# Gated attention and its feed-forward layer on one core: outputs split into a part by state and a part by scores, with the instruction order rebuilt

## The chip, the core and the metric

The kernel runs on one core of a Trainium2 chip. The core's engines are TensorE (PE in the profile; its weight loads are PEld), VectorE (DVE), ScalarE (ACT), GpSimd (POOL) and SyncE (SP), which issues all DMAs here. The metric is the device time of one execution in microseconds (us). Matmuls write to PSUM, which has eight banks; a bank is 512 fp32 wide on each of 128 partitions.

## What is computed

A gated linear attention over 4 batches, 8 heads, 768 steps and head size 48, then a feed-forward layer on the 3072 x 384 result:

```
for t in range(S):
    state = alpha[:, :, t, :, None] * state + np.einsum('bhd,bhe->bhde', k[:, :, t], v[:, :, t])
    y[:, :, t] = np.einsum('bhd,bhde->bhe', q[:, :, t], state)
...
h = x @ w_in                       # 3072 x 384 by 384 x 2048
g = np.where(pos, h, np.where(neg, 0.0, (h + beta) ** 2 / (4.0 * beta)))
return (g @ w_out).astype(np.float32)   # 3072 x 2048 by 2048 x 384
```

The two weight matrices come as 64-bit floats, the rest as fp32.

## The kernel before

**Chunks.** The steps are cut into 24 chunks of 128 (`NCH`; j counts them, six to a batch). A chunk is cut again into two halves u of 64 steps, and the 8 heads into 4 pairs g of two heads r. Head r of a pair lies on partitions 64r to 64r+47 (`low[r]`).

**Preparing a chunk** (`prepare`). SP loads alpha, k, q (L508 whole for the first `EARLY` chunks, L526 in four pieces for the later ones) and v (L577). The first `EARLY` chunks are transposed by the PE (L542, into PSUM), the later ones by DVE (L555). Two scans on DVE (L632, L658) make the decays, and products with them make Q (L678) and K (`inv`, L672).

**Attention of a chunk** (`begin_chunk`, `attend`). The PE transposes K (L699), and ACT copies the result to `ks` (L702). Three kinds of small fp32 matmuls follow, each on a part of the 128 x 128 array:

- `update` (L727): k^T v of a half u; rows of half u of the array, columns of head r, so the four quarter tiles of 64 x 64 take one each. A chunk that ends a batch has u = 0 alone.
- `scores` (L714): K with Q; rows of head r, columns of half u, again four quarter tiles.
- `outputs` (L854): the stationary operand is 128 rows of `both`, in which the state of a head (48 rows) and v (64 rows) lie above each other; the moving operand is Q for r = 0 and `other` for r = 1, each holding q on the rows of the state and masked scores on the rows of v. So each uses half of the array (all rows, 64 columns), and one matmul sums both parts.

Between them DVE multiplies the scores with the causal mask into the free rows of Q and `other` (L800, four of 64 partitions a chunk; for the first `HELP` chunks two of them go over ACT L772 and POOL L782), ACT copies Q's half into `other` (L764), DVE adds the update to `state` (L756), POOL decays it (L831), and ACT or POOL copies it into `both` (L746, L749), twice for each half. The output is then split into an fp32r high and low part in `ring` (L878 on ACT, L883 on DVE). From j = 7 (`MERGE`) the PE does update(j), scores(j) and outputs(j-1) as one burst; before that they are separate.

**Feed-forward** (`hidden`, `second`). Chunks go in groups of three (`GROUP`). A row f of a group is 128 of the 2048 hidden units: 9 matmuls of 128 x 384 (L950), the activation on ACT, DVE and POOL (L979, L994, L1005, L1009, L1010), and 9 matmuls (L1028). There are 8 groups of 16 rows f, so 128 rows L950 and 128 rows L1028, each counted here as one row of work. The first two groups take the first half of f before the second half. Weights come in eight pairs (SP L460, L470, L480) and are decoded to fp32r parts by ACT, DVE and POOL (L372 to L427). L994 is left out, and three ACT operations stand in its place, where a row's key is under `CLIPS`.

**What sets the order.** `Plan` records every operation with a duration, a key (its due time) and its operands, then places them engine by engine with its own costs of matmul modes, DMAs and waits, and emits the program in that order. Where it expects the PE to idle early on, it puts dummy matmuls in (L1099, `fill`). The constants at the top of the file steer it. Each engine works through its own row in that order.

## Time and profile before

| | |
|---|---|
| median of 3 runs | 530.55 us (530.52 to 531.27) |
| the profiled execution | 533.23 us, of which the profile's span is 531.5 us |
| PE busy by line, us (instructions, each of L714, L727 and L854 shown twice) | L1028 226.2 (x1152), L950 226.3 (x1188), L854 27.0 and 26.9 (x372 each) and 2.6 and 2.6 (x36 each), L714 16.6 (x768), L727 16.5 (x704), L1099 16.3 (x109), L699 14.7 (x96), L542 6.2, 6.1 and 5.9 (x36 each) |
| POOL, longest line | L1010 137.9 (x129) |
| DMA | 53.88 MB, 112241 packets, 77392 of them under 512 B |

The page of the profile gives busy time and share of the span for each engine, then the span in 40 slices (13.3 us each), the chain of work that ended last, and the groups of instructions by line with their mean duration. Matmuls overlap in the pipeline, so a row's duration is longer than the time from one matmul's start to the next.

### The profile page before, as it was taken

The numbers are of one execution on the slowest core, as the hardware profiler recorded it, in microseconds if no ns is written. First come the engines' busy times: TensorE is split into PE (matmuls) and PEld (weight loads), VectorE is DVE, ScalarE is ACT, GpSimd is POOL, SyncE is SP. The second block draws the span as 40 slices with busy tenths as digits, with TensorE's granted clock in tenths as the row PEclk, the third lists the DMA queues.
The fourth block names the chain that finished last, engine by engine and source line by source line (L and its number), as shares of the span: only waits on it lengthen the run. The fifth ranks groups of instructions, "written<-read, shape, count | busy, mean of one in ns | idle before, by whom it ended". The sixth has DMA issues, their size and how long they took to land.

```text
span 531.5 us, 12796 instructions
## 1 busy us (share of the span) xinstructions
PE 509.8 (96%) x4943; PEld 488.6 (92%) x4943; DVE 387.5 (73%) x709; ACT 281.0 (53%) x548; POOL 270.7 (51%) x327
## 2 busy tenths in 40 slices
PE   8888899999999999999999999999999999999995
PEld 6777789889989999999999999999999999999995
DVE  6799988778989896778686896688696884333331
ACT  3777898999845443434444543444444534334332
POOL 4656789879954443443543552543453552333330
PEclk9999999999999999999999999999999999999999
DMA  9999847892535733345324433345334210101001
GB/s 154 203 213 206 175 102 150 186 206 73 152 87 130 201 79 92 91 83 130 96 60 96 124 98 82 90 84 134 90 68 97 74 26 2 23 1 44 1 2 49
DMA packets 112241, 53.88 MB, mean 101 GB/s; under 512 B 77392, under 2 KB 107056, under 8 KB 112176
## 3 DMA queue, kind: packets, MB, share of 16 engines
q1 hardware_dynamic: 112176, 53.01, 44.9%
q8 instruction: 41, 0.67, 0.6%
q14 instruction: 24, 0.20, 0.1%
HBM read 45.02 MB, written 5.90 MB: 96 GB/s over the span
## 4 chain that ended last, share of the span: by engine, by line
PE 75%; DVE 7%; POOL 7%; ACT 3%; DMA 3%; issue 3%; SPq 1%; DVEq 0%; POOLq 0%
PE ps L1028 32%; PE ps L950 30%; PE ps L854 5%; PE ps L727 2%; PE ps L714 2%; POOL wt L427 2%; POOL gh L1010 2%; PE ps L699 2%; DMA sums<-ot 2%; PE ps L1099 1%; PE ps L542 1%; ACT gf L979 1%; DVE Q L632 1%; SPq L899 1%; POOL w L412 1%
## 5 line engine op out<-in xcount | busy, mean ns | idle before, releaser
L1028 PE MATMUL ps<-wt,gh 128*128 128x384 f32 x1152 | 226.2, 340 | 5.7 <-POOL gh L1010 3.4
L950 PE MATMUL ps<-ring,wt 128*128 128x384 f32 (+1 forms) x1188 | 226.3, 336 | 1.7 <-DMA ring<-ring 1.0
L1010 POOL TENSOR_TENSOR gh<-gf,gh 128x384 fp32r<-128x384 f32 (+1 forms) x129 | 137.9, 1070 | 158.1 <-ACT gh L1009 123.8
L950 PEld LDWEIGHTS ps<-ring,wt 128*128 128x128 f32 x1188 | 205.2, 188 | 4.0 <-issue 1.0
L1028 PEld LDWEIGHTS ps<-wt,gh 128*128 128x128 f32 x1152 | 200.2, 188 | 8.8 <-POOL gh L1010 5.3
L979 ACT ACTIVATE gf<-gf,half_b 128x384 f32<-128x384 f32 x104 | 63.8, 617 | 108.2 <-DVE gf L994 106.8
L1009 ACT CAST gh<-gf 128x384 fp32r<-128x384 f32 (+1 forms) x132 | 66.3, 503 | 77.7 <-DVE gf L1005 68.5
L1005 DVE TENSOR_TENSOR gf<-gf,ps 128x384 f32<-128x384 f32 (+1 forms) x132 | 70.3, 535 | 43.1 <-ACT gf L979 41.3
L994 DVE TENSOR_SCALAR gf<-ps 128x384 f32<-128x384 f32 x104 | 57.1, 552 | 52.1 <-PE ps L950 49.6
L427 POOL TENSOR_TENSOR wt<-w,wt 128x384 fp32r<-128x384 f32 x31 | 34.4, 1124 | 2.2 <-ACT wt L425 1.7
L831 POOL TENSOR_TENSOR state<-state,last 128x192 f32<-128x192 f32 x20 | 12.7, 634 | 36.1 <-DVE state L756 35.9
L412 POOL TENSOR_TENSOR w<-w,wt 128x384 int32<-128x384 int32 x26 | 28.5, 1114 | 5.1 <-issue 3.0
L854 PE MATMUL ps<-other,both 128*64 128x64 f32 x372 | 27.0, 225 | 0.0
L854 PE MATMUL ps<-Q,both 128*64 128x64 f32 x372 | 26.9, 225 | 0.0
L800 DVE TENSOR_TENSOR Q<-ps,mask 64x256 f32<-64x256 f32 x48 | 20.3, 423 | 8.3 <-ACT other L764 6.0
L854 PEld LDWEIGHTS ps<-Q,both 128*64 128x64 f32 x372 | 23.5, 138 | 2.5 <-issue 1.1
L632 DVE TENSOR_TENSOR_SCAN Q<-turn,fwd 128x512 f32<-128x512 f32 x15 | 21.0, 1399 | 6.6 <-PE ps L854 6.5
L702 ACT COPY ks<-ps 128x512 f32<-128x512 f32 x24 | 14.0, 584 | 20.1 <-PE ps L699 20.1
L678 POOL TENSOR_TENSOR Q<-Q,turn 128x512 f32<-128x512 f32 x16 | 20.7, 1294 | 6.8 <-DVE turn L555 6.4
L854 PEld LDWEIGHTS ps<-other,both 128*64 128x64 f32 x372 | 23.5, 138 | 0.0
L641 POOL TENSOR_SCALAR last<-Q 128x4 f32<-128x4 f32 x24 | 6.6, 274 | 28.6 <-DVE Q L632 28.1
L746 ACT COPY both<-state 48x192 f32<-48x192 f32 x51 | 17.8, 349 | 5.4 <-POOL state L831 3.9
(93 smaller groups left out, 570.3 us busy)
## 6 DMA issues: line engine op xcount, KB each, us to landing
wt<-in_moe_w_out SPq DMA_DIRECT2D x8, 768.0 KB, 7.5
raw_a<-in_alpha SPq DMA_DIRECT2D x60, 96.0 KB, 2.3
raw_k<-in_k SPq DMA_DIRECT2D x60, 96.0 KB, 2.4
raw_q<-in_q SPq DMA_DIRECT2D x60, 96.0 KB, 2.2
vt<-in_v SPq DMA_DIRECT2D x24, 192.0 KB, 4.0
wt<-in_moe_w_in SPq DMA_DIRECT2D x16, 288.0 KB, 5.8
out<-ot SPq DMA_DIRECT2D x24, 192.0 KB, 2.4
both<-in_v SPq DMA_DIRECT2D x72, 48.0 KB, 2.5
```

What stands on the lines that cost most here:

```text
L412: add = lambda e, c=c: e.tensor_tensor(out=bits()[:, c], in0=bits()[:, c], in1=word(I32, 0)[:, c], op=ALU.add)
L427: sub = lambda e, c=c: e.tensor_tensor(out=part(1)[:, c], in0=data()[:, c], in1=part(0).bitcast(F32)[:, c], op=ALU.subtract)
L632: lambda: nc.vector.tensor_tensor_scan(flat(Q()), aT(), flat(fwd), 0.0, ALU.mult, ALU.max),
L678: mul = lambda e: e.tensor_tensor(out=flat(Q()), in0=flat(Q()), in1=qT(), op=ALU.mult)
L854: nc.tensor.matmul(out=ps()[halves[r], to, halves[u]], lhsT=lhsT[:, u, r], rhs=x()[:, g, halves[u]], start=m + u == 0, stop=True, skip_gro ...
L950: nc.tensor.matmul(out=h(), lhsT=win(f, w)[:, kt], rhs=ring[:, at, kt, a, :], start=(m == 0), stop=(m == 3 * KT - 1),)
L979: lambda: nc.scalar.activation(out=gf(), in_=in_(), func=func, scale=scale, bias=bias),
L994: lambda: nc.vector.tensor_scalar(out=gf(), in0=h(), scalar1=-1.0, scalar2=1.0, op0=ALU.max, op1=ALU.min),
L1005: lambda: nc.vector.tensor_tensor(out=gf(), in0=gf(), in1=h(), op=ALU.max),
L1009: plan.op("ACT", 0.08 + 0.41 * w, key + 0.4, lambda: nc.scalar.copy(out=gh()[:, 0], in_=gf()), [gf], [gh])
L1010: sub = lambda e: e.tensor_tensor(out=gh()[:, 1], in0=gf(), in1=gh()[:, 0].bitcast(F32), op=ALU.subtract)
L1028: nc.tensor.matmul(out=o_ps[seg][t](), lhsT=gh()[:, a, (t - c0) * CH : (t - c0 + 1) * CH], rhs=wout(f, w), start=(f == f0 and i == 0), sto ...
```

## The change

Outputs are made in two passes that add up in PSUM. By state: `st` (48 rows of head r) with Q as it lies, into the columns of the same head, so quarter tiles on the diagonal of the array. By scores: `vv` (v of a half, on the rows of the other head) with `T`, the masked scores, so quarter tiles off the diagonal. A drain of the PE stands between. `T` is written by one DVE instruction for all 128 partitions, the state is added straight into `st`, and the copies into `both` and `other` are gone. A burst now also exists inside the first two groups (`joined`). The constants of the planner are changed, and its row of every engine is made anew. In the diff a line of "..." marks what is left out.

```diff
-EARLY = 9
+EARLY = 7
 MORE = 2
-WARM = 10
+WARM = 15
...
-MARGIN1 = 6.0
+MARGIN1 = 3.0
...
-LATER = 4.0
+LATER = 1.0
...
-HELP = 4
 VHELP = 6
-SPLIT = 2
-CLIPS = 24.0
+SPLIT = 1
+CLIPS = 9.0
...
-    ISSUE, LAND, RATE = 0.42, 1.9, 190e3
+    ISSUE, LAND, RATE = 0.42, 1.4, 300e3
+    SMALL = 2.1
...
-            vec(0.1, lambda: nc.vector.tensor_copy(out=meet[:, j, 1], in_=inv()[:, :, 0]), [inv], [("meet", j, 1)], False)
+            vec(0.15, lambda: nc.vector.reciprocal(out=meet[:, j, 1], in_=inv()[:, :, 0]), [inv], [("meet", j, 1)], False)
...
+        def joined(j):
+
+            return j + 1 < NCH and (j >= MERGE or group_of[j] == group_of[j + 1])
...
         def scores(j):
             Q, K, _ = prepared[j]
...
+            return [
+                lambda g=g, r=r, u=u: nc.tensor.matmul(
+                    out=meets[j][0]().rearrange("p (g t) -> p g t", g=G)[halves[1 - r], g, halves[u]],
+                    lhsT=K()[low[r], g, halves[u]],
+                    rhs=Q()[low[r], g, halves[u]],
...
+        def update(j, u):
+
+            return [
+                lambda g=g, r=r: nc.tensor.matmul(
+                    out=up(j, u)[64 * r : 64 * r + 64, g],
+                    lhsT=turnt[j]()[halves[u], g, 64 * r : 64 * r + 64],
+                    rhs=V[j]()[halves[u], 2 * g + r],
...
+        def outputs(j, ps, x):
+
+            n, i = group_of[j], j % 2
+            moving = (prepared[j][0], others[j])[x]
+            parts = [((st, vv)[x][:, i, :, g], g, g) for g in range(KT if n == 0 else G)]
+
+            parts += [((rest_s, rest_v)[x][:, :, kt], KT, kt) for kt in range(KT) if n == 0]
+
+            def product(m, u, r):
+                lhsT, g, to = parts[m]
+                rows = halves[1 - r] if x else low[r]
+
+                return nc.tensor.matmul(
+                    out=ps()[halves[r], to, halves[u]],
+                    lhsT=lhsT[rows, u],
+                    rhs=moving()[rows, g, halves[u]],
+                    start=m + u + x == 0,
...
+            return [lambda m=m, u=u, r=r: product(m, u, r) for m in range(len(parts)) for u in range(2) for r in range(2)]
+
+        def both(a, b):
+
+            todo = []
+            for i in range(0, max(len(a), len(b)), 2):
+                todo += a[i : i + 2] + b[i : i + 2]
+            return todo
...
         def follow(j, key):
...
-            plan.op("ACT", 0.6, key - 0.1, lambda: nc.scalar.copy(out=other()[HC:], in_=Q()[HC:]), [Q], [other])
...
+            plan.op(
+                "DVE",
+                0.66,
+                key,
+                lambda: nc.vector.tensor_tensor(
+                    out=T().rearrange("p g (u t) -> p (g u) t", u=2),
+                    in0=meets[j][0]().rearrange("p (g t) -> p g t", t=HC),
+                    in1=mask2[:, None, :].broadcast_to([P, 2 * G, HC]),
+                    op=ALU.mult,
+                ),
...
-                def burst(ps=ps):
-                    update(j)
-                    scores(j)
-                    outputs(j - 1, ps)
...
+            def burst():
+                more = update(j, 1) if (j + 1) % PER else []
+                if not before:
+                    run(scores(j) + both(update(j, 0), more))
+                    return
+                run(both(outputs(j - 1, old, 0), scores(j)))
+                run(update(j, 0))
+                nc.tensor.drain()
+                run(both(outputs(j - 1, old, 1), more))
...
+                def by_state():
+                    run(outputs(j, ps, 0))
+
+                def by_scores():
+                    nc.tensor.drain()
+                    run(outputs(j, ps, 1))
...
+        nc.vector.reciprocal(out=meet[:, :, 1], in_=meet[:, :, 1])
```

On the PE, in the middle of the program: the burst of chunk 11 before, a chunk that ends a batch (vt with ks is `update`, Q with inv is `scores`, Q or other with both is `outputs`). These are the first rows of it, after a row of the feed-forward; the last two repeat to sixteen.

```order
L950 MATMUL ps<-ring,wt 128x384 x9
L727 MATMUL ps<-vt,ks 64x48 x8
L714 MATMUL ps<-Q,inv 64x64 x16
L854 MATMUL ps<-Q,both 64x64
L854 MATMUL ps<-other,both 64x64
```

On the PE of the changed kernel, the middle of a burst of a chunk that does not end a batch, up to the feed-forward after it (Q with st is the pass by state, T with vv the pass by scores; the drain, which the rows do not name, stands behind the eight updates):

```order
L770 MATMUL ps<-Q,st 64x64 x2
L732 MATMUL ps<-Q,inv 64x64 x2
L747 MATMUL ps<-vt,ks 64x48 x8
L770 MATMUL ps<-T,vv 64x64 x2
L747 MATMUL ps<-vt,ks 64x48 x2
L770 MATMUL ps<-T,vv 64x64 x2
L747 MATMUL ps<-vt,ks 64x48 x2
L770 MATMUL ps<-T,vv 64x64 x2
L747 MATMUL ps<-vt,ks 64x48 x2
L770 MATMUL ps<-T,vv 64x64 x2
L747 MATMUL ps<-vt,ks 64x48 x2
L770 MATMUL ps<-T,vv 64x64 x8
```

The first two rows stand eight times in a burst. The sixteen outputs of before have become 32, the scores stand among the first sixteen, half of the updates stand alone, and the other half stand among the second sixteen.

On SP, which issues the DMAs: the rows before behind the third chunk's loads, where the fourth chunk's four loads come ahead of the second pair of weights.

```order
L508 DMA raw_a<-in_alpha 128x8x48
L508 DMA raw_k<-in_k 128x8x48
L508 DMA raw_q<-in_q 128x8x48
L577 DMA vt<-in_v 128x8x48
L460 DMA wt<-in_moe_w_in 48x3x256
L470 DMA wt<-in_moe_w_in 16x3x256
L460 DMA wt<-in_moe_w_in 48x3x256
L470 DMA wt<-in_moe_w_in 16x3x256
L480 DMA wt<-in_moe_w_out 128x2x384
```

The changed kernel there, from the last three rows of the second pair of weights to the fourth chunk's v; the third chunk's loads stand ahead of it:

```order
L469 DMA wt<-in_moe_w_in 48x3x256
L479 DMA wt<-in_moe_w_in 16x3x256
L489 DMA wt<-in_moe_w_out 128x2x384
L517 DMA raw_a<-in_alpha 128x8x48
L517 DMA raw_k<-in_k 128x8x48
L517 DMA raw_q<-in_q 128x8x48
L469 DMA wt<-in_moe_w_in 48x3x256
L479 DMA wt<-in_moe_w_in 16x3x256
L469 DMA wt<-in_moe_w_in 48x3x256
L479 DMA wt<-in_moe_w_in 16x3x256
L489 DMA wt<-in_moe_w_out 128x2x384
L586 DMA vt<-in_v 128x8x48
```

The second and third pair of weights have moved ahead of the fourth chunk's v. Further on, the fifth chunk's alpha, k and q follow, then the fourth pair of weights, then the fifth chunk's v.

More of the change, by code (lines that the diff above doesn't have):

```diff
@@ L279, in gated_attention_ffn @@
     )
+    mask2 = const.tile([P, HC], F32, name="mask2")
+    for u in range(2):
+        rows = slice(HC * u, HC * (u + 1))
+        nc.gpsimd.tensor_copy(out=mask2[rows], in_=mask[rows, rows])
+    st = const.tile([P, 2, 2, G, 64], F32, name="st")
+    rest_v = const.tile([P, 2, KT, 64], F32, name="rest_v")
+    rest_s = const.tile([P, 2, KT, 64], F32, name="rest_s")
     fwd = const.tile([P, G, CH], F32, name="fwd")
@@ L603, in prepare @@
                         lambda r=r, u=u, rows=rows: nc.sync.dma_start(
-                            out=both[rows, j % 2, u, :, r, 0:D],
+                            out=vv[rows, j % 2, u, :, 0:D],
                             in_=v[b, :, t0 + HC * u : t0 + HC * (u + 1), :].rearrange("(g r) s d -> r s g d", r=2)[r],
@@ L709, in scores, with run @@
+        def run(todo):
+            for f in todo:
+                f()
         def scores(j):
             Q, K, _ = prepared[j]
-            for g in range(G):
-                for r in range(2):
-                    for u in range(2):
-                        nc.tensor.matmul(
-                            out=ss(j, r)[halves[u], g],
-                            lhsT=K()[low[r], g, halves[u]],
-                            rhs=Q()[low[r], g, halves[u]],
-                            start=True,
-                            stop=True,
-                        )
@@ L722, in update @@
-        def update(j):
-            for g in range(G):
-                for u in range(1 + ((j + 1) % PER != 0)):
-                    for r in range(2):
-                        nc.tensor.matmul(
-                            out=up(j, u)[64 * r : 64 * r + 64, g],
-                            lhsT=turnt[j]()[halves[u], g, 64 * r : 64 * r + 64],
-                            rhs=V[j]()[halves[u], 2 * g + r],
-                            start=True,
-                            stop=True,
-                        )
@@ L735, in place @@
-        def place(i, u, key, zero=False):
-            for r in range(2):
-                to = both[low[r], i, u, :, r, 0:D]
-                if zero:
-                    plan.op("POOL", 0.15, key, lambda to=to: nc.gpsimd.memset(to, 0.0), [], [("s", i, u, r)])
-                    continue
-                plan.op(
-                    "ACT",
-                    0.36,
-                    key,
-                    lambda r=r, to=to: nc.scalar.copy(out=to, in_=state[low[r]]),
-                    ["state"],
-                    [("s", i, u, r)],
-                    other=("POOL", 0.38, lambda r=r, to=to: nc.gpsimd.tensor_copy(out=to, in_=state[low[r]]), True),
-                )
+            return [
[3 more added lines that the diff above has]
+                    rhs=Q()[low[r], g, halves[u]],
+                    start=True,
+                    stop=True,
+                )
+                for g in range(G)
+                for u in range(2)
+                for r in range(2)
+            ]
@@ L755, in grow @@
             else:
-                make = lambda: nc.vector.tensor_tensor(out=state, in0=state, in1=up(j, u), op=ALU.add)
-            plan.op("DVE", 0.33, key, make, [meets[j][u], "state"], ["state"])
+                make = lambda: nc.vector.tensor_tensor(out=to, in0=old, in1=up(j, u), op=ALU.add)
+            plan.op("DVE", 0.33, key, make, [*meets[j][1:], ("s", i, u)], [at])
         def follow(j, key):
             Q, _, last = prepared[j]
-            other = others[j]
+            T = others[j]
@@ L830, in follow @@
             grow(j, 1, key + 0.2)
+            new = st[:, 1 - i, 0, :, 0:D]
             decay = lambda e: e.tensor_tensor(
-                out=state, in0=state, in1=last()[:, :, None].broadcast_to([P, G, D]), op=ALU.mult
+                out=new, in0=new, in1=last()[:, :, None].broadcast_to([P, G, D]), op=ALU.mult
             )
@@ L838, in follow @@
                 lambda: decay(nc.gpsimd),
-                ["state", last],
-                ["state"],
+                [("s", 1 - i, 0), last],
+                [("s", 1 - i, 0)],
                 port=True,
@@ L928, in attend @@
-            follow(j, key)
-            if j < MERGE or j == NCH - 1:
-                ps = ps_a(j)
-                plan.op("PE", 1.0 + 0.5 * (group_of[j] == 0), key + 0.1, lambda ps=ps: outputs(j, ps), used(j), [ps], mode="col")
+            before = j > 0 and joined(j - 1)
+            old = ps_a(j) if before else None
+            load = 1 + 0.5 * (group_of[max(j - 1, 0)] == 0)
+            def burst():
[7 more added lines that the diff above has]
+                run(both(outputs(j - 1, old, 1), more))
@@ new lines, in attend @@
+            reads, writes = [Q, K, ks, vt], [*meets[j], others[j]]
+            if before:
+                reads, writes = [*reads, *used(j - 1, 0), *used(j - 1, 1)], [*writes, old]
+            plan.op("PE", 0.65 + (1.0 + 0.85) * load if before else 1.5, key, burst, reads, writes, mode="quad")
+            if before:
+                end_chunk(j - 1, old, key)
+            follow(j, key)
+            if not joined(j):
+                ps = ps_a(j)
+                wide = 1 + 0.5 * (group_of[j] == 0)
+                def by_state():
[3 more added lines that the diff above has]
+                    run(outputs(j, ps, 1))
+                plan.op("PE", 0.85 * wide, key + 0.1, by_state, used(j, 0), [ps], mode="quad")
+                plan.op("PE", 0.1 + 0.85 * wide, key + 0.1, by_scores, used(j, 1), [ps], mode="quad")
```

158 lines of the change are left out of this document (50 added, 108 removed).

## Prediction

> **What bounds the kernel now.** I read the page first, then busy times by stage, then the order of time on the PE. The page: busy time by engine, the span in 40 slices, the moved GB/s in the same slices, and the chain by engine.
>
> ```profile
> span 531.5 us, 12796 instructions
> PE 509.8 (96%) x4943; PEld 488.6 (92%) x4943; DVE 387.5 (73%) x709; ACT 281.0 (53%) x548; POOL 270.7 (51%) x327
> PE   8888899999999999999999999999999999999995
> DVE  6799988778989896778686896688696884333331
> PEclk9999999999999999999999999999999999999999
> GB/s 154 203 213 206 175 102 150 186 206 73 152 87 130 201 79 92 91 83 130 96 60 96 124 98 82 90 84 134 90 68 97 74 26 2 23 1 44 1 2 49
> PE 75%; DVE 7%; POOL 7%; ACT 3%; DMA 3%; issue 3%; SPq 1%; DVEq 0%; POOLq 0%
> ```
>
> The PE carries three quarters of the chain, at a full granted clock. The stages show where it is the bound; columns are the window, its length, then busy us and instructions of PE, PEld, DVE, ACT, POOL. I cut at 77.8 us, where the outputs of chunk 5 start, since they complete the second group's input.
>
> ```profile
> 45.90:77.80 31.90, 28.17 (x323) 24.63 (x322) 28.64 (x54) 29.47 (x63) 24.19 (x33) 1.00 0.81 157
> 77.80:115.70 37.90, 35.51 (x291) 33.86 (x291) 29.43 (x44) 34.98 (x61) 31.12 (x31) 1.00 0.84 181
> 115.70:165.00 49.30, 47.50 (x525) 45.72 (x524) 43.03 (x71) 36.33 (x68) 39.27 (x44) 1.00 0.44 111
> 165.00:448.00 283.00, 282.03 (x2742) 275.13 (x2737) 221.14 (x420) 122.61 (x244) 125.08 (x145) 1.00 0.38 92
> ```
>
> From 77.8 to 448 us the PE is idle for 2.4 + 1.8 + 1.0 = 5.2 us in all, so there a us of PE work is a us of time, and work taken from DVE, ACT or POOL (221, 123 and 125 us of the 283 in the long stage) gives nothing back. Before 77.8 us all engines share the bound.
>
> **The price of a burst.** One steady burst, in order of time (start, duration of the run, line, count). The PE's record shows each fp32 matmul twice: 16 instructions are x32.
>
> ```profile
> 242.42 0.60 PE L699 MATMUL ps<-ident,inv 128*128 128x128 f32 x4
> 242.77 1.29 PE L1028 MATMUL ps<-wt,gh 128*128 128x384 f32 x6
> 243.99 0.68 PE L727 MATMUL ps<-vt,ks 64*64 64x48 f32 x32
> 244.50 0.66 PE L714 MATMUL ps<-Q,inv 48*64 48x64 f32 x32
> 245.09 0.27 PE L854 MATMUL ps<-Q,both 128*64 128x64 f32 x1
> ...
> 245.19 0.22 PE L854 MATMUL ps<-Q,both 128*64 128x64 f32 x1
> 245.20 0.22 PE L854 MATMUL ps<-other,both 128*64 128x64 f32 x1
> ...
> 246.01 0.22 PE L854 MATMUL ps<-Q,both 128*64 128x64 f32 x1
> 246.02 0.22 PE L854 MATMUL ps<-other,both 128*64 128x64 f32 x1
> 246.17 0.80 PE L1028 MATMUL ps<-wt,gh 128*128 128x384 f32 x3
> ```
>
> Outputs start in pairs, one for each half of the array, 14 steps from 245.19 to 246.01: a round takes 0.0586 us. Updates and scores: 32 records in 0.51 and 0.59 us, that is eight rounds of four quarter tiles (8 x 0.0586 = 0.47) and a remainder at the change of kind. What a round costs when fewer tiles are named is shown by chunk 5, which has updates of one half alone, on the two upper tiles:
>
> ```profile
> 70.15 0.67 PE L727 MATMUL ps<-vt,ks 64*64 64x48 f32 x16
> 70.75 0.33 PE L542 MATMUL ps<-ident,raw_a 128*128 128x128 f32 x1
> 83.45 0.68 PE L727 MATMUL ps<-vt,ks 64*64 64x48 f32 x32
> 84.06 0.45 PE L1028 MATMUL ps<-wt,gh 128*128 128x384 f32 x1
> ```
>
> 16 records on two tiles take 0.60 us to the next run, 32 on four tiles 0.61. So **a tile takes one record each 0.0586 us, whatever the others do**, and time is counted in rounds of the busiest tile. Before, a burst is 8 + 8 + 16 = 32 rounds, 1.88 us, and 246.17 - 243.99 = 2.18 us in all; 0.30 us go to the entry, the change of tile shape at the outputs (about 0.12) and the way back (0.15).
>
> The changed burst by the code and its rows. First part: sixteen outputs by state on the diagonal tiles between sixteen scores on the other two, eight instructions a tile: 16 rounds. Second: eight updates of u = 0 on the two upper tiles: 8 rounds, lower tiles empty. Drain. Third: outputs by scores use upper right and lower left, but the updates of u = 1 need lower left and lower right. **Lower left gets 8 + 4 = 12 instructions, 24 rounds.** Sum 48 rounds, 2.81 us. For the gaps: 0.30 less 0.12 for the shape that no longer changes, and a drain. No row shows one; its bounds are 0 (the wait hidden) and 0.36 (a whole matmul of 0.22 behind the last start, and a weight load of 0.14 before the next), the nearest row being the change of shape at 246.02 to 246.17, 0.15, which I take. Burst after: 2.81 + 0.18 + 0.15 = 3.14, **+0.96 us**. Without u = 1 (chunks 11, 17, 23) the third part is 16 rounds: 2.67 against 2.16, +0.51.
>
> The Trainium skill, page TensorEngine Tiling (Array Packing), section Key Properties, says that changing the tiling mode drains the TensorE; the 0.15 us above agree, and by it the burst saves one such drain and gets one back.
>
> **Sum from the outputs of chunk 5 to the end.** By the rows of both kernels 17 bursts (chunks 7 to 23) follow, at nearly the same places in the feed-forward: 14 x 0.96 + 3 x 0.51 = +15.0. The last chunk's own outputs were 16 rounds and 0.15, and become 32 rounds, 0.15 and a drain with its entry 0.2: +1.15. Chunk 5's own the same: +1.15. Six PE transposes of four (chunks 7 and 8) go to DVE, at 0.35 us each by the row at 242.42 to 242.77 and 0.05 for the change of work: -2.4. At this milestone the new order has done 13 rows of feed-forward (8 of L949, 5 of L1027), the old one 11 (7 and 4). Two rows of the chain in order of time, and the PE's row at the milestone (start, duration, line, count):
>
> ```profile
> 168.49 1.57 PE ps L950 x9
> 170.06 1.57 PE ps L1028 x9
> 77.82 0.27 PE L854 MATMUL ps<-Q,both 128*64 128x64 f32 x1
> ```
>
> A row is 1.57 us, so -3.1. Before, 531.5 - 77.8 = 453.7; after 453.7 + 15.0 + 1.15 + 1.15 - 2.4 - 3.1 = 465.5.
>
> **When the milestone comes.** Group means, and the DMA issues with KB each and us to landing:
>
> ```profile
> L800 DVE TENSOR_TENSOR Q<-ps,mask 64x256 f32<-64x256 f32 x48 | 20.3, 423 | 8.3 <-ACT other L764 6.0
> L883 DVE TENSOR_TENSOR ring<-ps,ring 128x512 fp32r<-128x512 f32 (+1 forms) x24 | 15.9, 661 | 1.8 <-ACT ring L878 1.6
> L994 DVE TENSOR_SCALAR gf<-ps 128x384 f32<-128x384 f32 x104 | 57.1, 552 | 52.1 <-PE ps L950 49.6
> L764 ACT COPY other<-Q 64x512 f32<-64x512 f32 x24 | 14.8, 616 | 0.6
> L746 ACT COPY both<-state 48x192 f32<-48x192 f32 x51 | 17.8, 349 | 5.4 <-POOL state L831 3.9
> L555 DVE STREAM_TRANSPOSE turn<-raw_a 128x512 f32<-128x512 f32 x15 | 16.5, 1100 | 0.0
> wt<-in_moe_w_out SPq DMA_DIRECT2D x8, 768.0 KB, 7.5
> vt<-in_v SPq DMA_DIRECT2D x24, 192.0 KB, 4.0
> wt<-in_moe_w_in SPq DMA_DIRECT2D x16, 288.0 KB, 5.8
> ```
>
> The one mask instruction should cost what L883 does, 0.66 (same shape, also from PSUM). For chunks 0 to 5 the DVE's masks go from 16 x 0.42 = 6.8 to 4.0 us, and ACT loses 16 x 0.35 of state copies and 6 x 0.62 of Q copies, 9.3 us. That is a real relief. But data come later. A pair of weights is 768 + 2 x 288 + 2 x 96 KB = 1.57 MB, a chunk 4 x 192 KB = 0.79 MB. In the new SP order chunk 4's v stands behind five chunks and four pairs, 3.93 + 6.29 = 10.2 MB. At the GB/s row's 154, 203, 213 and 206 in slices of 13.3 us that is reached at 52.7 us; before, with two pairs ahead of it, 7.1 MB at 37.5. I keep the rate, the queue being full then. Chunk 4's burst can then start at about 53.5. Behind it on the PE stand, up to the outputs of chunk 5: that burst 3.1, six rows 9.4, transposes of two chunks and of K 2.8, chunk 5's burst 2.7: 71.5 us with no wait. In 45.9 to 77.8 the PE now idles 31.9 - 28.2 = 3.7 us; I keep 3.5, so **75 us** (71.5 to 80). Span 75 + 465.5 = 540.5, +9.0.
>
> Costed at nothing: the mask, state and copy edits after 77.8 us and the reciprocal for `meet` at the end, beside DVE's idle time; they would only show if the DVE were late for a burst. CLIPS of 9 puts some 14 L994 (0.55) on DVE between chunks 6 and 7 and the stream transposes of chunks 7 and 8 put six L555 (1.1) there, 14 us against some 5 us of masks saved and 8.5 us idle in 77.8 to 115.7: it just fits. If not, the decode of late weights is late next.
>
> The profiled execution took 533.2 us with 1.7 us around the span; the median is 530.55, so I add +9.0 to that: **539.5 us**.
>
> **Rivals.**
> - *The tiles pack fully*: the shared lower-left tile and the empty lower half cost nothing, a burst stays at 32 rounds. Then 14 x 0.94 + 3 x 0.47 = 14.6 us less: 525, faster. It decides if two instructions on one tile overlap. The 16 records in 0.60 us speak against it. Chance 0.08. The same page of the Trainium skill, same section, says that different tiles can execute in parallel; no row here shows two on one tile doing so.
> - *The head gains what the bursts lose*: relief of DVE and ACT brings the milestone to 70 us, and the 5.2 us of idle PE shrink by 4: 530.5, from 526 to 533. It needs the queue to deliver chunk 4's v before 50 us. Chance 0.09.
> - *The late weights starve the PE*: the 14 us more on DVE delay the decode in 77.8 to 165 us, idle PE doubles (+5): 545, to 553 with a milestone at 80. Decides where POOL and DVE are both full. Chance 0.13.
> - *Row tiles take turns in a bank*: upper and lower tiles now write the same bank, in different partitions, which before they never did. If served in turn, the first part takes 32 rounds and the third 40, +32 rounds, 1.9 us a burst, +33: 572. Chance 0.04. The page named above, section Gotcha 1: PSUM Pressure, says different row tiles cannot access one bank at the same time; no run here shows what that does to time.
>
> **How the numbers follow.** Forecast 0.66, its own range 534 to 546: milestone 72 to 79, drain 0 to 0.36 over 19 drains (-2.9 to +4.0). The range 530 to 550 takes in the starving case and the upper half of the second rival, and leaves out full packing, turns in a bank, and tails, under 0.2. Faster by over 0.2% (what a measurement here can tell from none): 0.08 and half of 0.09, 0.13; same 0.05; slower 0.82.
>
> **What would show it.** In the changed trace: the distance from a burst's first output to the next feed-forward row (3.1 us; 2.2 for full packing, 5 for turns); rounds in the third part, first at double pace, then single; start of chunk 5's outputs by state (75); idle PE from there to 448 us (5). The forecast fails if bursts take under 2.6 us, or if the milestone lies before 66.

## The result and the profile after

The changed kernel takes 546.25 us (median of 4 runs, 544.97 to 548.08), the kernel before beside it 530.91 us (4 runs): a ratio of 1.0285, 95% interval 1.0258 to 1.0313. It is slower, inside the predicted range (530 to 550), 6.75 us above the predicted 539.5 and just outside the forecast's own range (534 to 546). The profiled execution is the fastest of the four, 544.97 us with a span of 543.2.

The page of the profile after, the lines that answer to those shown of before:

```profile
span 543.2 us, 14089 instructions
PE 525.8 (97%) x5692; PEld 506.4 (93%) x5692; DVE 367.1 (68%) x656; ACT 234.5 (43%) x437; POOL 257.8 (47%) x290
PEclk9999998899999999999999999999999999999999
GB/s 160 203 239 204 211 194 138 271 112 62 117 130 85 168 122 50 73 134 99 70 112 33 142 128 31 89 118 98 86 102 44 83 31 1 23 1 45 2 0 48
```

DVE, ACT and POOL lost 20, 46 and 13 us of work and the PE gained 16. In two slices, 81 to 109 us, the granted clock (PEclk, the share of its full speed at which the PE was let run) falls below nine tenths, which it never did before.

The stages after (window, length, busy us and instructions of PE, PEld, DVE, ACT, POOL, then granted clock, DMA share, GB/s). The long stage is cut at 460 us, as the end came later:

```profile
45.90:77.80 31.90, 30.90 (x448) 28.72 (x447) 28.68 (x52) 28.83 (x54) 27.43 (x34) 1.00 1.06 207
77.80:115.70 37.90, 33.31 (x325) 30.85 (x325) 26.40 (x43) 20.73 (x36) 22.74 (x23) 0.91 0.81 196
115.70:165.00 49.30, 48.41 (x450) 47.20 (x448) 45.96 (x72) 23.83 (x44) 41.05 (x35) 1.00 0.37 100
165.00:460.00 295.00, 293.64 (x3301) 286.45 (x3295) 202.32 (x374) 104.29 (x198) 114.43 (x118) 1.00 0.36 86
```

The head (what lies ahead of some 78 us) is fuller, and the stage behind it is emptier: from 77.8 us on the PE is idle for 4.6 + 0.9 + 1.4 = 6.9 us, against 5.2 before. Not all of that is waiting. The PE's groups from 73.7 us to the end, with the idle time before them behind the last bar and what ended it:

```profile
L1027 PE MATMUL ps<-wt,gh 128*128 128x384 f32 x1107 | 218.2, 340 | 3.4 <-ACT gh L1008 2.1 <-POOL wt L436 0.8 <-POOL gh L1009 0.5
L949 PE MATMUL ps<-ring,wt 128*128 128x384 f32 x1081 | 211.5, 341 | 1.9 <-DMA ring<-ring 1.9
L770 PE MATMUL ps<-T,vv 64*64 64x64 f32 x608 | 28.2, 227 | 1.6
```

The 1.6 us before the outputs by scores belong to the 19 drains, some 0.08 us each, and so to the price of a burst. The waits are 3.4 + 1.9 = 5.3 us, hardly more than before.

One burst in order of time (start, duration of the run, line, count), chosen in the long stage:

```profile
266.57 0.27 PE L770 MATMUL ps<-Q,st 48*64 48x64 f32 x2
266.59 0.27 PE L732 MATMUL ps<-Q,inv 48*64 48x64 f32 x2
...
267.56 0.63 PE L747 MATMUL ps<-vt,ks 64*64 64x48 f32 x16
268.27 0.28 PE L770 MATMUL ps<-T,vv 64*64 64x64 f32 x2
268.29 0.25 PE L747 MATMUL ps<-vt,ks 64*64 64x48 f32 x1
...
269.23 0.64 PE L770 MATMUL ps<-T,vv 64*64 64x64 f32 x15
269.80 1.84 PE L1027 MATMUL ps<-wt,gh 128*128 128x384 f32 x9
```

From the first output to the next feed-forward row: 3.23 us (2.17 before). The outputs by state beside the scores take 0.99 (16 rounds of 0.0586 are 0.94), the eight rounds of updates and the drain 0.71, so **the drain's gap is 0.24** (0.71 less 8 x 0.0586), and the third part 1.53: slow, 0.96, while the updates of u = 1 stand between its outputs, then the rest at the pace of pairs.

Where the outputs of chunk 5 start, and what the PE waits for behind them:

```profile
73.69 1.15 PE L770 MATMUL ps<-Q,st 48*64 48x64 f32 x32
...
84.64 0.77 PE L949 MATMUL ps<-ring,wt 128*128 128x384 f32 x3 [1.47 <-DMA ring<-ring]
85.85 4.44 PE L949 MATMUL ps<-ring,wt 128*128 128x384 f32 x14 [0.45 <-DMA ring<-ring]
...
97.94 0.62 PE L1027 MATMUL ps<-wt,gh 128*128 128x384 f32 x2 [2.11 <-ACT gh L1008]
99.04 2.12 PE L1027 MATMUL ps<-wt,gh 128*128 128x384 f32 x7 [0.47 <-POOL gh L1009]
```

The wait at 98 us leads through ACT's own order of work:

```profile
90.81 0.51 ACT L1008 CAST gh<-gf 128x384 fp32r<-128x384 f32 x1 [0.62 <-DVE gf L1004]
95.10 0.90 ACT L389 ACTIVATE wt<-wt 128x768 int32<-128x768 uint32 x1 [3.78 <-DMA wt<-in_moe_w_in]
95.90 0.61 ACT L978 ACTIVATE gf<-gf,half_b 128x384 f32<-128x384 f32 x1
```

L389 is the first look at a pair of weights that has not landed; the square of a feed-forward row (L978) stands behind it in ACT's row and cannot pass. And windows of 2 us after each wait show the clock:

```profile
86.00:88.00 2.00, 2.00 (x6) 1.49 (x7) 0.78 (x2) 0.00 (x0) 0.00 (x0) 0.50 0.38 61
88.00:90.00 2.00, 2.00 (x10) 2.00 (x9) 0.00 (x0) 1.53 (x3) 0.00 (x0) 0.65 0.52 86
...
100.00:102.00 2.00, 2.00 (x8) 2.00 (x8) 1.08 (x2) 0.46 (x1) 2.00 (x3) 0.50 1.01 284
102.00:104.00 2.00, 2.00 (x11) 2.00 (x9) 0.81 (x2) 1.32 (x3) 0.94 (x1) 0.74 1.04 394
```

The PE is busy there at half its clock: in these windows and 98 to 100 us (clock 0.91) 2 x (0.50 + 0.35 + 0.50 + 0.26 + 0.09) = 3.4 us are lost without showing as idle time.

### The profile page after: what moved, and what is told of

Read it like the earlier page. It is cut to its first block, busy times and chain, and to the rows that moved or that the text cites. A ratio compares the mean times of both kernels' runs of the same rounds, so it can differ in the third digit from the quotient of the medians.

```text
span 543.2 us, 14089 instructions
## 1 busy us (share of the span) xinstructions
PE 525.8 (97%) x5692; PEld 506.4 (93%) x5692; DVE 367.1 (68%) x656; ACT 234.5 (43%) x437; POOL 257.8 (47%) x290
## 4 chain that ended last, share of the span: by engine, by line
PE 77%; DVE 7%; POOL 4%; DMA 3%; SPq 3%; ACT 3%; issue 3%; DVEq 0%; ACTq 0%; POOLq 0%
PE ps L1027 32%; PE ps L949 31%; PE ps L770 8%; DMA wt<-in_moe_w_in 2%; PE ps L747 2%; POOL gh L1009 2%; PE ps L712 2%; POOL wt L436 1%; DVE w L408 1%; DVE Q L641 1%; ACT w L381 1%; DVE inv L667 1%; SPq L469 1%; POOL w L421 1%; DMA vv<-in_v 1%
## 5 line engine op out<-in xcount | busy, mean ns | idle before, releaser
L1009 POOL TENSOR_TENSOR gh<-gf,gh 128x384 fp32r<-128x384 f32 (+1 forms) x127 | 137.3, 1081 | 198.5 <-ACT gh L1008 155.4
L978 ACT ACTIVATE gf<-gf,half_b 128x384 f32<-128x384 f32 x119 | 73.3, 617 | 138.7 <-DVE gf L993 129.4
L1008 ACT CAST gh<-gf 128x384 fp32r<-128x384 f32 (+1 forms) x130 | 65.9, 508 | 92.4 <-DVE gf L1004 76.8
L770 PE MATMUL ps<-T,vv 64*64 64x64 f32 x744 | 34.6, 227 | 2.1
L770 PEld LDWEIGHTS ps<-T,vv 64*64 64x64 f32 x744 | 31.4, 133 | 5.0 <-issue 5.0
L869 DVE TENSOR_TENSOR ring<-ps,ring 128x512 fp32r<-128x512 f32 (+1 forms) x24 | 16.1, 673 | 29.0 <-ACT ring L864 29.0
L747 PE MATMUL ps<-vt,ks 64*64 64x48 f32 x704 | 34.6, 220 | 0.0
L838 POOL TENSOR_TENSOR st<-st,last 128x192 f32<-128x192 f32 x20 | 16.0, 798 | 35.9 <-DVE st L796 35.7
L747 PEld LDWEIGHTS ps<-vt,ks 64*64 64x64 f32 x704 | 30.6, 134 | 0.0
L770 PEld LDWEIGHTS ps<-Q,st 48*64 48x64 f32 x744 | 23.6, 134 | 5.8 <-issue 5.5
L732 PE MATMUL ps<-Q,inv 48*64 48x64 f32 x768 | 27.6, 221 | 0.0
L770 PE MATMUL ps<-Q,st 48*64 48x64 f32 x744 | 26.9, 221 | 0.0
L732 PEld LDWEIGHTS ps<-Q,inv 48*64 48x64 f32 x768 | 24.3, 134 | 0.7 <-issue 0.4
```

The source lines that it names most:

```text
L732: lambda g=g, r=r, u=u: nc.tensor.matmul(out=meets[j][0]().rearrange("p (g t) -> p g t", g=G)[halves[1 - r], g, halves[u]], lhsT=K()[low[r ...
L747: lambda g=g, r=r: nc.tensor.matmul(out=up(j, u)[64 * r : 64 * r + 64, g], lhsT=turnt[j]()[halves[u], g, 64 * r : 64 * r + 64], rhs=V[j]() ...
L770: return nc.tensor.matmul(out=ps()[halves[r], to, halves[u]], lhsT=lhsT[rows, u], rhs=moving()[rows, g, halves[u]], start=m + u + x == 0, ...
L978: lambda: nc.scalar.activation(out=gf(), in_=in_(), func=func, scale=scale, bias=bias),
L1008: plan.op("ACT", 0.08 + 0.41 * w, key + 0.4, lambda: nc.scalar.copy(out=gh()[:, 0], in_=gf()), [gf], [gh])
L1009: sub = lambda e: e.tensor_tensor(out=gh()[:, 1], in0=gf(), in1=gh()[:, 0].bitcast(F32), op=ALU.subtract)
```

## The experiments

Each time stands beside runs of the kernel before on the same chip, with the ratio and its 95% interval. Where a term is read from the profiled execution, it is "from the milestone to the end": the span less the start of chunk 5's outputs. Before that is 531.5 - 77.8 = 453.7, after 543.2 - 73.7 = 469.5.

### Structure and order apart: e3 and e4

e3 is the changed kernel with the constants and estimates of the order as they were, e4 the kernel before with the new ones (the same lines, the other way round):

```diff
-EARLY = 7
+EARLY = 9
-WARM = 15
+WARM = 10
-MARGIN1 = 3.0
+MARGIN1 = 6.0
-LATER = 1.0
+LATER = 4.0
-SPLIT = 1
-CLIPS = 9.0
+SPLIT = 2
+CLIPS = 24.0
-    ISSUE, LAND, RATE = 0.42, 1.4, 300e3
-    SMALL = 2.1
+    ISSUE, LAND, RATE = 0.42, 1.9, 190e3
...
                 wire = max(wire, t) + o.moved / self.RATE
-                t = wire + self.LAND
+                t = max(wire, t + self.LAND)
...
```

> The changed kernel's arithmetic (outputs by state and by scores apart, drain, one mask instruction, state and Q as they lie) with the constants of the order as they were before (EARLY 9, WARM 10, MARGIN1 6, LATER 4, SPLIT 2, CLIPS 24, the old estimates of landing and rate). Theory (the loss is in the bursts, 16.7 us in the long part and 1.2 at each end, and the constants gain about what they lose): 546 to 550, bursts of 3.2 us, and less loss in 81 to 104 us. Rival (the new constants cause the loss of 9 us in 81 to 104 us, which the old ones did not have): 537 to 541. Second rival (the new constants are what gains the 7 us up to the milestone): 551 to 555.

> The kernel before, whole arithmetic and bursts as they were, with the new constants and estimates of the order. Theory (constants gain up to the milestone and lose it in 81 to 104 us): 529 to 533, bursts of 2.2 us, the granted clock falling below .9 somewhere in 80 to 105 us. Rival (the loss in 81 to 104 us comes with the constants, while the head's gain comes with the fewer DVE and ACT instructions): 536 to 542. Second rival (the constants are a gain by themselves): 523 to 527.

| | old order | new order |
|---|---|---|
| old structure | 530.8 | e4: 545.06, 1.0277 (1.0248 to 1.0307) |
| new structure | e3: 550.39, 1.0375 (1.0334 to 1.0416) | after: 546.25, 1.0285 (1.0258 to 1.0313) |

e3 lies at the slow edge of its theory (546 to 550), with bursts of 3.23 us as expected. Its milestone comes at 73.65 us, as in the changed kernel, but with 9 rows of the feed-forward done in place of 13. The stage behind it loses less:

```profile
77.80:115.70 37.90, 37.14 (x342) 35.48 (x343) 33.67 (x46) 33.98 (x60) 31.25 (x31) 1.00 0.99 215
```

So the new order gains four rows (6.3 us) in the head and pays part of that back behind it, as e3's theory has it.

In the old order the new structure costs 19.6 us, hardly more than its bursts (16.7 us) and own outputs (2.5) count, so no gain from its relief of DVE and ACT shows there. In the new order it costs 1.2. The new order costs the old structure 14.2 us and gains the new one 4.1. So **neither half's effect is its own**, and no theory named e4's 545. Its PE waits:

```profile
51.56 0.24 PE L855 MATMUL ps<-Q,both 128*64 128x64 f32 x1 [3.13 <-DVE inv L659]
95.17 1.30 PE L951 MATMUL ps<-ring,wt 128*128 128x384 f32 x3 [5.11 <-DMA ring<-ring]
136.70 1.94 PE L1029 MATMUL ps<-wt,gh 128*128 128x384 f32 x7 [2.11 <-POOL gh L1011]
```

Three different releasers, 3.1, 5.1 and 2.1 us. The first and the last are engines from which the new structure takes work, so one reading is that the old structure's DVE and POOL are late for an order made for less work; e4 alone does not show that. The next run puts such work back into the changed kernel.

### The relief taken back: e9

```diff
+                nc.scalar.copy(out=Q()[HC:], in_=Q()[HC:])
-                nc.vector.tensor_tensor(out=T()..., in1=mask2 ...)      # 128 x 512
+                for v in halves:
+                    for u in halves:
+                        nc.vector.tensor_tensor(out=T()[v, :, u], ...)  # 64 x 256
...
+                for r in range(2):                                      # in grow
+                    nc.scalar.copy(out=to[low[r]], in_=to[low[r]])
```

> The changed kernel with the work that it takes off DVE and ACT put back at the same places of the same order: the mask as four instructions of 64 x 256 in place of one of 128 x 512, for each chunk a copy of half of Q (onto itself) and four copies of the state (onto themselves) on ACT. The outputs stay the reference's. The prediction's step (these edits are worth something only in the head, nothing once the feed-forward feeds the PE): from chunk 7's burst to the end 430 us as in the changed kernel, within 1; up to there 2 to 5 us later: 548 to 551. Rival (they are worth nothing at all, since the head waits for transfers): within 1.5 us of 546. Second rival (they carry the long stage too, since T and the state are late for the bursts): over 555.

557.67 us, 1.0496 (1.0464 to 1.0528): 11.4 us over the changed kernel, more than twice what was expected. Where:

```profile
84.89 0.33 PE L770 MATMUL ps<-Q,st 48*64 48x64 f32 x3
...
124.16 0.27 PE L770 MATMUL ps<-Q,st 48*64 48x64 f32 x2
```

The milestone comes at 84.9 in place of 73.7 us, chunk 7's burst at 124.2 in place of 113.0. From there to the end it is 556.3 - 124.2 = 432.1 us against 543.2 - 113.0 = 430.2, 1.9 more where at most 1 was expected. By the medians 11.4 - 1.9 = 9.5 us fall to the head (the profile's own 11.2 holds some of the spread between executions, below). So **with this work put back the kernel loses some 9.5 us in the head and 1.9 behind it**, in this order. For the relief itself that is likely too much, since e9's copies stand where they hold ACT up more than those of the kernel before did. Its copies of the state up to 78 us, in e9 and before (the idle time of ACT before them behind the last bar):

```profile
L801 ACT COPY st<-st 48x192 f32<-48x192 f32 x20 | 7.0, 350 | 5.5 <-DVE st L794 3.1 <-DVE st L796 2.1
L746 ACT COPY both<-state 48x192 f32<-48x192 f32 x16 | 5.6, 348 | 1.1 <-DVE state L754 0.7 <-POOL state L831 0.3
```

And 3.4 us of the loss up to chunk 7's burst are clock: e9 has four drops to half the clock up to there, of 3.4 us each, the changed kernel two.

### Rounds, or the drain: e1 and e10

e1 splits the updates another way around the drain: the quarters that cross go ahead of it, those on the diagonal stand beside the outputs by scores, on tiles that these leave free. e10 drains twice.

```diff
 # e1
                 run(both(outputs(j - 1, old, 0), scores(j)))
-                run(update(j, 0))
+                a = update(j, 0)
+                off = [f for ab in zip(a[1::2], more[0::2]) for f in ab] if more else a[1::2]
+                on = [f for ab in zip(a[0::2], more[1::2]) for f in ab] if more else a[0::2]
+                run(off)
                 nc.tensor.drain()
-                run(both(outputs(j - 1, old, 1), more))
+                run(both(outputs(j - 1, old, 1), on))
 # e10
                 nc.tensor.drain()
+                nc.tensor.drain()
```

> The changed kernel with the updates split another way around the drain: ahead of it go the updates whose rows and partitions cross (u=0 with r=1 on the upper right tile, u=1 with r=0 on the lower left), behind it, beside the outputs by scores, the other two quarters, which lie on the diagonal tiles. Work, drains and order of all else stay. Theory of rounds (a tile takes one pass per 0.0586 us, the busiest tile of a part sets its length): 16 + 8 + 16 = 40 rounds in place of 48, a burst 3.23 - 0.47 = 2.76 us, the part behind the drain about 1.1 us in place of 1.53; the bursts without u=1 stay at 2.77. 14 x 0.47 = 6.6 us off 546.2: 539 to 540.5. Rival (the burst is long because of the drain and of the lone two-tile stretch, not because of the shared tile): a burst stays above 3.1 us and the time within 1 us of 546. Second rival (rounds fall, but the PE then waits for DVE and late weights in 80 to 105 us): bursts of 2.76 in the long stage, but less than 5 us gained.

> The changed kernel with a second drain behind the one in every joined burst (17 bursts from chunk 7 on, and those of the head). Theory (the 0.24 us between the updates and the third part are the emptying of the array, which a second drain finds empty): a burst grows by at most 0.06 us, 1 us in all, 546 to 548. Rival (a drain costs its 0.24 us by itself): bursts of 3.47 us, 17 x 0.24 = 4.1 us more, 550 to 551.5.

e1: 540.84 us, 1.0195 (1.0165 to 1.0226), 5.4 us under the changed kernel. A burst of it:

```profile
265.88 0.27 PE L770 MATMUL ps<-Q,st 48*64 48x64 f32 x2
...
266.88 0.62 PE L747 MATMUL ps<-vt,ks 64*64 64x48 f32 x16
...
268.10 0.64 PE L770 MATMUL ps<-T,vv 64*64 64x64 f32 x16
268.67 1.83 PE L1030 MATMUL ps<-wt,gh 128*128 128x384 f32 x9
```

268.67 - 265.88 = 2.79, for the same instructions and the same drain: 0.44 less, where 0.47 was expected. The time lies 0.3 us over the 539 to 540.5 of the theory. **The rounds of the busiest tile set a burst.** 14 x 0.44 are 6.2 us; from the milestone to the end this profile has 539.0 - 74.9 = 464.1 us in place of 469.5, 5.4 less. These do not match term by term: the PE's waits from there on grew from 5.3 to 6.6 us, one of the changed kernel's two drops to half the clock (1.7 us) is gone, and about 1 us is not assigned. Most of the growth is this wait, 2.11 us before:

```profile
98.99 0.62 PE L1030 MATMUL ps<-wt,gh 128*128 128x384 f32 x2 [3.14 <-ACT gh L1011]
```

e10: 549.02 us, 1.0347 (1.0314 to 1.0379). The gap it bears on:

```profile
269.74 0.62 PE L747 MATMUL ps<-vt,ks 64*64 64x48 f32 x16
270.53 0.28 PE L770 MATMUL ps<-T,vv 64*64 64x64 f32 x2 [0.17 <-issue]
```

0.79 us from the updates to the third part in place of 0.71: a second drain costs 0.08 us, a little over the 0.06 expected. The other 0.16 of the first one's 0.24 are not paid a second time, as they should not be if they are the wait for the matmuls ahead of it; the rival (0.24 for each drain) is out. 17 x 0.08 = 1.4 us; the median rose by 2.8, and the rest is not assigned. From the milestone to the end this profile has 469.5 us, as the changed kernel: it has the 1.4 us more and one drop to half the clock (1.7 us) less.

### The waits of 85 and 98 us: e2, e5, e6, e7, e8

e2 makes the last two pairs of weights due earlier on SP, and the planner then orders the other engines anew too (ACT does 434 instructions in place of 437). e5 and e6 move single rows and nothing else: e5 the four L389 of these pairs later on ACT, e6 chunk 7's q behind the transfers of the ring on SP. e7 is both, e8 both with e1.

```diff
 # e2
-            fetch = key - (FETCH if u else FETCH0)
+            fetch = key - (FETCH if u else FETCH0) - 3.0 * (u > 5)
 # e5 (LATE = 6.0): L389 of the last two pairs
-                )
+                ).late = LATE * (u > 5)
 # e6: the transfers of raw_q
-                    )
+                    ).late = 4.0 * (j == 7 and x == "q")
 # e5 and e6, at the end of order()
-        return done
+        for o in done: o.place = max([o.start + getattr(o, "late", 0.0), *(d.place + 1e-6 for d in o.deps)])
+        return sorted(done, key=lambda o: o.place)
```

> The changed kernel with the due time of the transfers of the last two pairs of weights 3 rows earlier, so that they stand ahead of chunk 8's alpha, k and q on SP's queue and one of the two ahead of the ring's transfers; nothing else is edited. Theory (the 9 us lost in 81 to 104 us come from weights that land at 92 to 103 us, which block ACT's queue, make the PE wait and lower its granted clock): the PE's wait of 2.1 us at 98 us goes, the granted clock stays above .9 in 96 to 104 us, 3 to 5 us gained: 541 to 543. Rival (those losses belong to the ring's transfers and to DVE, which holds 14 us more of work there): the PE waits as long at another instruction, the time within 1.5 us of 546. Second rival (a pair of weights ahead of the ring's transfers delays the second group's input): slower, 547 to 550.

> The changed kernel with one thing moved: the four instructions of ACT (L389) that read the last two pairs of weights first stand 6 us of the planner's time later in ACT's queue, behind the squares and casts of three to four rows of feed-forward; the order on PE, DVE, POOL and SP is the same as in the changed kernel. Theory (ACT's queue is blocked by weights that land at 95 and 101 us, so the feed-forward's own casts are late; the PE then waits 2.11 + 0.47 us at 98 us and runs at a granted clock of .50 to .74 in 100 to 104 us): the wait goes, the clock stays above .9 there, 2.6 + 1.7 = 4.3 us gained, 541 to 543. Rival (the weights are late for the PE themselves, or DVE is): the wait moves to a later row, within 1 us of 546.

> The changed kernel with one thing moved: the four transfers of chunk 7's q (needed at 91 us by DVE) stand behind the six transfers inside the ring on SP's queue, so these are issued 1.9 us earlier; no other engine's order changes. The PE's wait of 1.47 + 0.45 us at 85 us should shrink to below 0.3 and the granted clock stay above .9 in 86 to 90 us. Theory (the next wait, at 98 us, is set by the landing of weights at 95 us, whatever the PE does before): what is gained at 85 us is lost again there, within 1 us of 546. Rival (each wait costs by itself): 1.9 + 1.7 us gained, 542 to 543.

> Both moves together (chunk 7's q behind the ring's transfers on SP, the decode of the last two pairs later on ACT). Theory: neither wait is left, granted clock 1.0 from 80 to 160 us, 4.0 + 4.3 us gained, 537 to 540. Rival (a wait for data takes their place, at the next thing that lands): 541 to 543, as with the decode alone.

> Both moves and the crossed updates of e1 (bursts of 40 rounds, 2.78 us). If the three gains add: 546.2 - 8.3 - 6.3 = 531.6, 530 to 534, about the time of the kernel before. Rival (the shorter bursts only reach the late weights sooner): 535 to 537.

The last two columns hold, from the milestone on, the PE's waits (its idle time less the drains) and what the drops to half the clock cost, in us:

| | us | ratio | milestone | to the end | waits | low clock |
|---|---|---|---|---|---|---|
| after | 546.25 | 1.0285 (1.0258 to 1.0313) | 73.7 | 469.5 | 5.3 | 3.4 |
| e2 | 552.52 | 1.0389 (1.0352 to 1.0425) | 76.9 | 475.0 | 9.1 | 5.1 |
| e5 | 547.92 | 1.0310 (1.0287 to 1.0332) | 79.7 | 469.5 | 6.1 | 1.7 |
| e6 | 547.21 | 1.0327 (1.0280 to 1.0374) | 76.1 | 469.4 | 6.7 | 3.4 |
| e7 | 548.75 | 1.0322 (1.0301 to 1.0342) | 79.2 | 470.5 | 5.1 | 5.1 |
| e8 | 542.32 | 1.0214 (1.0188 to 1.0240) | 74.4 | 466.3 | 7.2 | 3.4 |

In e5 and e6 the wait that was aimed at went, and none of the moves gained anything: only e8 is faster than the changed kernel, by e1's shorter bursts. In e6 the ring's wait is gone and the next one grew:

```profile
100.31 3.70 PE L1027 MATMUL ps<-wt,gh 128*128 128x384 f32 x9 [5.81 <-ACT gh L1008]
```

That is the theory of e6. In e5 the wait at 98 is gone, and this stands in its place, first on DVE, then on the PE:

```profile
113.01 1.12 DVE L564 STREAM_TRANSPOSE turn<-raw_a 128x512 f32<-128x512 f32 x1 [5.68 <-DMA raw_a<-in_alpha]
```

```profile
114.57 0.67 PE L747 MATMUL ps<-vt,ks 64*64 64x48 f32 x16 [0.53 <-DVE gf L1004]
130.31 0.62 PE L1027 MATMUL ps<-wt,gh 128*128 128x384 f32 x2 [2.17 <-ACT gh L1008]
```

DVE's row is blocked by chunk 8's alpha as ACT's was by weights. In e7 the PE stands still for longer, inside chunk 7's burst:

```profile
114.39 0.67 PE L747 MATMUL ps<-vt,ks 64*64 64x48 f32 x16 [2.30 <-DVE gf L1004]
```

The theory behind e5, e7 and e8 (each wait costs by itself) fell: 4.3, 8.3 and 8.3 us were expected from the moves, and none came; e8 is even 1.5 us over e1, and 2.2 us (466.3 against 464.1) from the milestone on. e2 is slower than its slowest rival, and hardly by that mechanism: the ring's wait is little longer (2.05 us), but others came:

```profile
127.91 2.38 PE L1027 MATMUL ps<-wt,gh 128*128 128x384 f32 x7 [2.33 <-POOL gh L1009]
...
139.14 2.61 PE L1027 MATMUL ps<-wt,gh 128*128 128x384 f32 x7 [2.30 <-POOL gh L1009]
```

POOL did not wait in its turn. Ahead of the second L1009 its row holds four instructions of the decode of weights:

```profile
131.84 5.37 POOL L421 TENSOR_TENSOR w<-w,wt 128x384 int32<-128x384 int32 x4
137.18 1.91 POOL L1009 TENSOR_TENSOR gh<-gf,gh 128x384 fp32r<-128x384 f32 x1
```

And on SP e2 did less than its expectation says. In the changed kernel both late pairs already stood ahead of chunk 8's alpha, behind chunk 7's alpha, k and q and the ring. In e2 one pair moved ahead of these; the other still stands behind them (issued at 93.14 us, 90.86 in the changed kernel). So e2 shows what another order of all engines did, and not what earlier weights are worth.

### What the stage waits for: e11 and e12

e11 takes 15 clips off DVE. e12 leaves out the ten transfers of the last two pairs of weights (3.15 MB) and decodes the raw tiles of the two pairs before a second time; the order of PE, ACT, DVE and POOL is that of the changed kernel, SP's lacks the ten rows.

```diff
 # e11
-CLIPS = 9.0
+CLIPS = 24.0
 # e12, in weights(u)
+            if u > 5:
+                ti, to = kept[u - 2]
+            kept[u] = ti, to
...
+            real = lambda emit: emit if u < 6 else lambda: None
```

> The changed kernel with CLIPS back at 24, which takes 15 clips of 0.55 us from DVE between 80 and 165 us and gives ACT two more instructions for each of these rows. Theory (77 to 165 us is bound by what lands when: weights, chunk 8's alpha): within 1.5 us of 546. Rival (DVE, 46 of 49 us busy in 115 to 165 us, is the bound there, as the rival of the starving weights has it): 3 to 5 us faster, 541 to 543. Second rival (ACT's queue, blocked by late weights, gets worse): 549 or more.

> The changed kernel without the ten transfers of the last two pairs of weights (3.15 MB); in their place the raw tiles of the two pairs before are decoded a second time, so that all decoding, all feed-forward and the order on every engine stay, and SP's queue loses these ten rows. The outputs are not the reference's. Theory (what lands when sets the stage of 77 to 165 us: with the late weights gone, chunk 8's data come 10 us earlier too): the wait at 98 us and the low clock after it go and no other takes their place; from the start of chunk 5's outputs to the end 462 to 466 us in place of 469.5, the time 538 to 543. Rival (DVE, POOL and ACT set it with their decode, so a wait for them appears at 110 to 145 us as in e5 and e7): 468 to 470 from there, 545 to 548.

e11: 550.83 us, 1.0374 (1.0345 to 1.0404), slower, the second rival. With more to do ACT's row is later (a wait of 2.48 us for L1008 at 128 us). The gain that DVE as the bound was to bring did not come, but the run does not part the two cleanly, since the work went to ACT. That DVE was not the bound is better read from the changed kernel: none of the 5.3 us of waits behind its milestone was ended by DVE, and the longest leads to a transfer.

e12: 543.07 us, 1.0232 (1.0190 to 1.0274), 3.2 us under the changed kernel, 0.07 over the 538 to 543 expected. Its milestone is at 75.5 us, and from there to the end it takes 539.9 - 75.5 = 464.4 us in place of 469.5. The stage and the PE's waits in it:

```profile
77.80:115.70 37.90, 36.48 (x374) 34.53 (x371) 31.88 (x49) 24.24 (x41) 26.71 (x27) 1.00 0.49 121
```

```profile
85.92 1.41 PE L956 MATMUL ps<-ring,wt 128*128 128x384 f32 x6 [0.92 <-DMA ring<-ring]
87.74 3.92 PE L956 MATMUL ps<-ring,wt 128*128 128x384 f32 x21 [0.41 <-DMA ring<-ring]
```

No wait is left at 98 us, no other takes its place up to 112 us, the clock stays at 1.00 and the DMA share falls from 0.81 to 0.49. Chunk 8's alpha is issued at 90.68 us in place of 98.86. From the milestone on the PE's waits fall from 5.3 to 2.7 us and the 3.4 us of low clock are gone, 6.0 in all; 5.1 were gained, and 0.6 of the difference lie behind the PE's last matmul. So **the landing of data sets the stage of 77 to 115 us**: some 5 us from the milestone on. In e5, e6 and e7 the order only chose which engine's row is blocked.

None of the twelve beat the kernel before; e1, at 540.84 us, is the best of them.

## Why the prediction was right, and where it was off

- **The price of a burst** was right in kind: 16 + 8 + 24 rounds, with the lower left tile as the busiest. Forecast 3.14, measured 3.23; the 0.09 is the drain, for which the prediction took "the nearest row being the change of shape at 246.02 to 246.17, 0.15", and which took 0.24, inside its bounds. Over 14 bursts and three of 2.77 (+0.61): 16.7 in place of 15.0 us. e1 shows that it is the rounds.
- **Own outputs**: 2.32 us in place of 1.08 (73.69 to 76.01, and the last chunk's the same), +1.24 against +1.15.
- **The milestone** was to come at 75 us (71.5 to 80). It came at 73.7 here; in e5, e6, e7 and e12, which run the same order up to there, at 79.7, 76.1, 79.2 and 75.5. The gate that the forecast named, chunk 4's v, had landed at 52.45 us, with 52.7 forecast, and chunk 4's burst started at 53.62, with 53.5 forecast, behind a row of the feed-forward and without a wait:

```profile
52.45 1.62 POOL L605 COPY vv<-vt 64x192 f32<-64x192 f32 x2 [0.35 <-DMA vt<-in_v]
53.62 0.27 PE L770 MATMUL ps<-Q,st 48*64 48x64 f32 x2
```

From there to the milestone the PE was busy for 19.2 us and idle for 0.9, where the prediction had 18.0 and 3.5: two misses that cancel in part, which is luck.

- **Idle PE from there on** was kept at the 5.2 us of before, and the waits are 5.3, at other places. What failed is a term that the prediction does not have: the clock. It counted on full clock throughout, and 3.4 us went at half clock after the waits at 85 and 98 us. With it, 0.1 us of waits and 0.3 for chunk 6's scores and updates (1.53 us in one run, 0.63 and 0.61 before), 453.7 + 16.7 + 2.5 - 2.4 - 3.1 = 467.4 becomes 471.2, and 469.5 were measured. Of the 1.7 us between, 0.8 lie behind the PE's last matmul (4.9 us to the end of the span, 5.6 before); 0.9 are not assigned.
- **"Costed at nothing"** held behind the head within 1.9 us (e9). In the head the relief was called real, but only the queue was reckoned with, and e9 puts the relief at some 9.5 us, likely too much: with the work put back the milestone is at 85, not 75. The forecast counted PE work and transfers alone, and never asked whether DVE and ACT could keep up there. That they could is a condition that it left out.
- **"It just fits. If not, the decode of late weights is late next"**: no wait of the PE behind the milestone was ended by DVE, which is busy for 26.4 of the 37.9 us in 77.8 to 115.7, and the late weights were late all the same. The prediction looked for them behind DVE; they stood behind chunk 7's alpha, k and q and the ring on SP, and the ACT instruction that waited for them held up the feed-forward. The rival of the starving weights (545 to 553) named the place and the price, but not the cause: idle PE did not double, and the 3.4 us lost are clock.
- **The last step, adding the span's difference to the median**, cost more than all else. The profiled executions differ by 544.97 - 533.23 = 11.7 us, 2.7 over the forecast of 9.0; the medians by 15.3. The kernel before was profiled in an execution 2.3 us above its median, the changed one in the fastest of its four, 1.3 below: 3.6 us that no step of the sum is about.

Of the rivals, full packing and turns in a bank are out by the rows: 0.99 us for the first part, 16 rounds, neither 8 nor 32. The head that gains what the bursts lose is out too: it needed a milestone at 70 us and chunk 4's v before 50, and neither came. In that first part upper and lower tiles write the same bank, in different partitions, at full pace. The Trainium skill, page TensorEngine Tiling (Array Packing), section Gotcha 1: PSUM Pressure, says that row tiles cannot access one bank at the same time; by these rows that does not hold for time where their partitions differ.

What stays open: why the milestone of one order moves by 6 us between executions, and how much of the head's gain is the relief and how much the order, since e9 gives the first only roughly.

## What to carry to other kernels

Price a group of small matmuls by the tile that gets the most of them, and look for a split that evens the tiles out before looking at barriers: here that was 0.44 us a burst, and the barrier 0.24. A wait of a busy engine behind a queue of transfers is not a gain in store: before moving what waits, ask what lands next, and try it by leaving the transfer out. Constants of a planner that were fitted to one amount of work are part of that work; test both halves of such a change apart, and compare medians with medians.

## What the runs showed of the hardware

The granted clock fell to 0.50 after short waits. Of 22 single waits of the PE of 2.0 us or more in the changed kernel and the experiments, 19 were overlapped, or followed within 2 us, by 3.4 us at 0.50 (14 of them) or by 6.8 (5); 2.05 (e2), 2.34 (e8) and 2.48 (e11) were not. Of 14 waits of 1.2 to 2.0 us, all five of before among them, one was, and a wait of 0.45 stood close behind that one; three more drops followed several shorter waits. Such a drop costs 1.7 us, nearly as much as the wait. The Trainium skill, page TensorE: Matmul & The Clock Gate, section Part 1: The HAM clock gate (the "warmup" mystery), gives a free-running window of 3.4 us and a drop after at least one idle window. The traces agree with the window: the drops are 3.41 or 6.83 us long, and within a run they begin whole multiples of 3.41 us apart (13.65 in the changed kernel, 4 times; 40.96 and 44.37 in e4, 12 and 13 times). That equal waits differ fits a window that runs freely; but here 2.02 us of waiting sufficed.

A second drain right behind a first cost 0.08 us, and two instructions on different row tiles that write one bank in different partitions started together at every round of 0.0586 us.
